# Turning q and k by DMA transposes from the sixth unit on, in a fused attention and Mish MLP kernel

## The chip, the cores and the metric

The kernel runs on one NeuronCore of a Trainium2 chip. The metric is the device time of one execution in microseconds (us), lower is better. A profile of one execution is read beside it; in it PE is TensorE (matmuls and transposes through the array), PEld its weight loads, DVE is VectorE, ACT is ScalarE, POOL is GpSimd, and SP is SyncE, which here only issues DMAs, one after the other in program order.

## The reference

Attention with one added to the softmax's denominator, followed by a two-layer network with the Mish activation. q, k and v have 8 batches, 12 heads, 448 rows and 64 columns.

```python
scores = scale * np.matmul(q, k.transpose(0, 1, 3, 2))
m = np.max(scores, axis=-1, keepdims=True)
e = np.exp(scores - m)
attn = e / (np.sum(e, axis=-1, keepdims=True) + np.exp(-m) + 1e-09)
attn_out = np.matmul(attn, v)
...
x = attn_out.transpose(0, 2, 1, 3).reshape(B * S, H * D)      # 3584 x 768
h = x @ w_in                                                  # 768 x 2048
sp = np.where(h > 20.0, h, np.log1p(np.exp(np.minimum(h, 20.0))))
out = (h * np.tanh(sp)) @ w_out                               # 2048 x 768
```

## The kernel before

The 12 heads of a batch are taken as 6 pairs (`HP`), so that 2 x 64 columns fill the 128 partitions, and there are 48 pairs in all (`N_PAIRS`). Three pairs make a unit (`UNIT_PAIRS`), two units a batch, 16 units the whole. The 448 rows of a head are loaded as 112 partitions with 4 row groups (`NT`, `SP_`).

For each pair, q, k and v are loaded by SP (`load_pair`, line 148, three DMAs of 224 KB) and cast to bf16 by POOL (`cast_pair`, lines 192 to 198, and `cast_v`, line 178). Then q and k have to be turned, so that the 64 columns of each head lie on partitions. `transpose_pair` (line 215) does that with eight PE transposes of 112 x 128 into PSUM, and `evac_qk` (lines 255 and 263) copies the two results into a tile `qkT` (DVE takes q and multiplies by the scale, ACT takes k). `turn_by_dma` (line 229) does it with two DMA transposes issued on SP instead, straight from the cast tiles to `qkT`; for such pairs the scale goes into the cast of q (line 194). `rest_of` (lines 237 and 238) then has POOL copy the last 64 rows of q of both heads into a small tile.

`scores` (lines 293 to 301) multiplies q with k, and DVE takes the row maxima (line 319). `exps` (line 330) is the exponential on ACT into the tile `en`. `denominators` and `normalise` (lines 343 to 366) divide: two pairs of a unit on DVE, the third on POOL (line 364). `normalise` also issues the DMA transpose of `en` into `eT` on SP (line 370), 128 x 3584 in bf16. `av_pair` (line 403) multiplies `eT` with v into `xT`. `mm1_mish` (lines 422 and 450) is the first layer with Mish into `gT`, and `mm2_part` (line 511) the second layer, whose results are copied out by DVE (line 498) and stored by SP (`store_rows`, line 476).

The order on each engine is the order in which the code emits instructions (`manual_schedule`). The main loop goes over units. A unit has a body of twelve steps, each with the exponentials of one score block, and between them the scores that come next, the products with v of the unit before, and pieces of the second layer, by a table written out by hand (`GROUPED`, line 553). In the body SP also gets the three pairs' loads (steps 0, 3 and 6, `LOAD_AT`) and the turns by DMA (steps 8 and 11, `TURN_AFTER`, line 704); POOL gets the casts of the first two of the next unit's pairs. After it comes a tail of eight steps, each with one block of the first layer: step 0 normalises the first pair, steps 1, 3 and 5 turn the next unit's three pairs on PE unless they are turned by DMA, step 1 casts the next unit's third pair, step 3 has `rest_of` for pairs turned by DMA and normalises the second pair, step 4 normalises the third on POOL, and step 7 emits the first scores of the next unit.

So SP sees for each unit: three transposes of `en`; then nine loads with two or four stores among them (their places repeat every four units); then, where pairs are turned by DMA, two transposes for each, the first pair's behind the last loads, the second's behind a store that may follow. `qkT` has three buffers, `eT` three, the cast q and k six, and `en` four.

Of the kernel before, what the change touches and what calls it, by code (L numbers as in the profile page):

```python
# [15 lines left out]
UNIT_PAIRS = 3  # L16
# [3 lines left out]
def kernel(  # L20
# [27 lines left out]
    N_PAIRS = B * HP  # L48
# [62 lines left out]

    GROUP_FROM = 2 * HP
    ONE_COPY = range(1, HP + UNIT_PAIRS)
    TURN_BY_DMA = (N_PAIRS - UNIT_PAIRS, N_PAIRS - UNIT_PAIRS + 1)
    SCALED_IN_CAST = (*ONE_COPY, *TURN_BY_DMA)
    q_rests = [
        singles.tile([128, 2, 64], BF16, tag=f"qr{i}", name=f"qr{i}") for i in range(UNIT_PAIRS)
# [53 lines left out]
    def load_w(n):  # L171
        for _ in range(min(n, len(pieces))):
            dst, src = pieces.popleft()
            nc.gpsimd.dma_start(out=dst, in_=src.rearrange("(a p) c -> p a c", p=128))
# [28 lines left out]
    def transpose_pair(p, bank=None):  # L203
        if p >= N_PAIRS:
            return
        q_bf, k_bf, _ = casted[p]
        ps = mo_take() if bank is None else sc_banks[2][bank]
        ps_k = sc_banks[1][bank] if bank is not None else mo_take() if p == 0 else ps
        by_s = [
            t[:, :].bitcast(BF16).rearrange("p (s n) -> p s n", s=2)[:, s, :]  # L210
            for s, t in enumerate((ps, ps_k))
        ]
        for s, src in enumerate((q_bf, k_bf)):
            for t in range(NT):
                nc.tensor.transpose(  # L215
                    by_s[s][:, t * SP_ : (t + 1) * SP_],
                    src[:, t].rearrange("p h d -> p (h d)"),
                    ident[:SP_, :SP_],
                )
        own = [] if bank is not None else [ps, ps_k] if p == 0 else [ps]  # L220
        if p in ONE_COPY:
            by_s = ps[:, :].bitcast(BF16).rearrange("p (s n) -> p s n", s=2)[:, :, 0:S]
        qkT[p] = (by_s, own)

    def turn_by_dma(p):
        qk = qk_pool.tile([128, 2, S], BF16, tag="qkT", name="qkT")
        pair = qk[:, 0, :], qk[:, 1, :]
        for dst, src in zip(pair, casted[p]):
            nc.sync.dma_start_transpose(
                out=dst.rearrange("c (t q) -> c t q", q=SP_),  # L230
                in_=src.rearrange("q t h d -> q (t h d)"),
            )
        qkT[p] = pair
# [115 lines left out]
    def normalise(p, dma=True, on_pool=False, shared=0):  # L349
        st = att[p]  # L350
        en = st["en"]
        by_pool = range(NTILE) if on_pool else range(shared)
        for i in [*(i for i in range(NTILE) if i not in by_pool), *by_pool]:
            pool_does = i in by_pool
            if pool_does and i == 0:

                st["rden2"] = st_pool.tile([128, NTILE], FP32, tag="rden2", name="rden2")
                nc.vector.tensor_copy(out=st["rden2"], in_=st["rden"])  # L358
            args = dict(
                out=en[:, :, i, 0:SP_], in0=en[:, :, i, 0:SP_],  # L360
                scalar1=st["rden2" if pool_does else "rden"][:, i : i + 1],
            )
            if pool_does:
                nc.gpsimd.tensor_scalar(scalar2=1.0, op0=ALU.mult, op1=ALU.mult, **args)  # L364
            else:
                nc.vector.tensor_scalar(scalar2=None, op0=ALU.mult, **args)  # L366
        eT = eT_pool.tile([128, NT, 2 * S], BF16, tag="eT", name="eT")
        st["eT"] = eT
        if dma:
            nc.sync.dma_start_transpose(  # L370
                out=eT.rearrange("c j (i q) -> c (j i) q", q=128),
                in_=en.rearrange("q j i c -> q (j i c)"),
            )
# [284 lines left out]
    for u in range(UNITS_PER_B, N_UNITS + 2 * UNITS_PER_B):  # L658
# [12 lines left out]
        for n in range(steps):  # L671
            pi, s = divmod(n, STEPS)
            p, idx = p0 + pi, p0 * STEPS + n
# [4 lines left out]
            if grouped:  # L678
# [23 lines left out]
                if u - UNITS_PER_B < len(W_AT):  # L702
                    load_w(W_AT[u - UNITS_PER_B].get(n, 0))
                if n in TURN_AFTER and nxt + TURN_AFTER.index(n) in TURN_BY_DMA:
                    turn_by_dma(nxt + TURN_AFTER.index(n))
# [40 lines left out]
        for f in range(FF_U):  # L746
# [20 lines left out]
            if f in (1, 3, 5):  # L767
                if nxt + f // 2 not in TURN_BY_DMA:
                    transpose_pair(nxt + f // 2, bank=f // 2 % 2)
# [7 lines left out]
            if f == 3:  # L777
                normalise(todo[1], dma=todo[1] not in BY_PE)
                for p in TURN_BY_DMA:
                    if p // UNIT_PAIRS == u + 1:  # L780
# [42 lines left out]
```

## Time and profile before

| | us |
|---|---|
| three runs | 462.74, 466.14, 467.04 (median 466.14) |
| the profiled execution, from its first to its last instruction | 465.8 |
| ACT busy in it | 347.0 |
| DVE busy | 338.1 |
| POOL busy | 184.9 |
| landing of a q, k, v load after its issue (median) | 4.9, 5.3, 5.4 |
| landing of an `eT` transpose (median of 43) | 6.7 |
| landing of a `qkT` transpose, q and k (median of 2 each) | 5.9, 4.7 |

Rows of the profile name line, engine and operation, then what is written and read, the shapes and the count. In a group's row follow busy time and the mean time of one in ns, then the engine's idle time before them and what ended it. In a timeline the first two numbers are start and length in us, and a row on SP ("SPq") is the time that the issue of a DMA took, not its transfer; idle time before an instruction and its cause stand in brackets at the end. A row of the stretches gives a window, its length, the busy time and instruction count of each engine (PE, PEld, DVE, ACT, POOL), the granted TensorE clock as a share, the DMA engines' busy share and GB/s. A line of forty digits gives the busy tenths in forty equal slices of the span.

### The profile page before, as it was taken

Reading aid. Unit: us, or ns where it says so; the run is one execution under the profiler, and the core shown is the slowest. Engines: PE = TensorE matmul, PEld = TensorE weight load, DVE = VectorE, ACT = ScalarE, POOL = GpSimd, SP = SyncE. Lnnn points to the kernel's source line nnn. Section 1 sums busy time; section 2 is a strip of 40 time slices with the busy share of each in tenths; the row PEclk is TensorE's granted clock in tenths of the full one; section 3 lists DMA queues with packets and bytes.
Section 4 is the critical chain, followed back from the end, with each engine's and each line's share of the span. In section 5 each row is a group of like instructions: output and inputs, shape, how many; then the busy total and the mean of one; then the engine's idle time right before and its main releaser. Section 6 shows DMA issues by size and latency. Waiting matters only on the chain.

```text
span 465.8 us, 8846 instructions
## 1 busy us (share of the span) xinstructions
PE 439.0 (94%) x3032; PEld 235.2 (51%) x3032; DVE 338.1 (73%) x728; ACT 347.0 (74%) x916; POOL 184.9 (40%) x352
## 2 busy tenths in 40 slices
PE   4587899899999999999999999999999999999996
PEld 2243545454445454645555554545454555555565
DVE  4899767878887878878796888788787979430121
ACT  5998877889796979889796969798887969311300
POOL 4666828362617253444536271625354350000000
PEclk9997699899999999999999999999999999999999
DMA  8999999998999999898999989999999995950213
GB/s 224 218 193 230 255 160 237 201 184 198 205 244 228 247 199 213 231 207 246 201 239 211 250 137 251 216 224 225 197 232 216 233 207 126 172 136 1 68 35 101
DMA packets 204300, 90.81 MB, mean 195 GB/s; under 512 B 160992, under 2 KB 200800, under 8 KB 204256
## 3 DMA queue, kind: packets, MB, share of 16 engines
q1 hardware_dynamic: 196672, 83.92, 84.0%
q0 software_dynamic: 7488, 6.29, 9.2%
q8 instruction: 23, 0.38, 0.3%
q14 instruction: 21, 0.17, 0.1%
q10 hardware_dynamic: 96, 0.05, 0.0%
HBM read 45.61 MB, written 11.01 MB: 122 GB/s over the span
## 4 chain that ended last, share of the span: by engine, by line
PE 76%; DVE 8%; ACT 7%; DMA 4%; issue 3%; POOL 1%; SPq 1%; POOLq 0%; ACTq 0%; DVEq 0%
PE mo L511 30%; PE mo L422 22%; PE b L403 6%; PE b L422 6%; DVE negm L319 6%; ACT en L330 6%; DMA k_f<-in_k_dram 4%; PE b L293 3%; PE sc L293 2%; PE sc L215 2%; PE b L215 1%; PE mo L403 1%; PE mo L301 1%; DVE eT L385 1%; PE mo L381 1%
## 5 line engine op out<-in xcount | busy, mean ns | idle before, releaser
L511 PE MATMUL mo<-w_out_sb,gT 128*128 128x384 bf16 (+1 forms) x896 | 141.5, 304 | 0.9 <-DVE o_sb L498 0.7
L422 PE MATMUL mo<-xT,w_in_sb 128*128 128x448 bf16 x600 | 125.6, 353 | 0.6 <-ACT gT L450 0.3
L511 PEld LDWEIGHTS <-gT 128*128 128x128 bf16 x896 | 80.2, 98 | 58.8 <-issue 20.2
L450 ACT ACTIVATE gT<-mo 128x448 bf16<-128x448 f32 x98 | 53.3, 544 | 69.7 <-PE mo L422 69.3
L422 PEld LDWEIGHTS <-w_in_sb 128*128 128x128 bf16 x768 | 71.7, 98 | 64.6 <-issue 6.7
L330 ACT ACTIVATE en<-sc,negm 128x448 bf16<-128x448 f32 x156 | 97.6, 640 | 7.4 <-DVE negm L319 6.1
L319 DVE TENSOR_REDUCE negm<-b 128x1 f32<-128x448 f32 x144 | 79.9, 617 | 22.2 <-PE b L296 22.2
L319 DVE TENSOR_REDUCE negm<-sc 128x2 f32<-128x896 f32 x84 | 84.5, 1018 | 7.0 <-PE sc L296 3.7
L330 ACT ACTIVATE en<-b,negm 128x448 bf16<-128x448 f32 x144 | 89.5, 650 | 0.0
L364 POOL TENSOR_SCALAR en<-en,rden 128x448 bf16<-128x448 bf16 x109 | 67.3, 635 | 33.0 <-DVE rden L358 22.8
L366 DVE TENSOR_SCALAR en<-en,rden 128x448 bf16<-128x448 bf16 x227 | 68.0, 370 | 0.7
L498 DVE COPY o_sb<-mo 128x384 f32<-128x384 f32 (+1 forms) x64 | 32.3, 504 | 48.3 <-PE mo L511 44.5
L192 POOL CAST q_bf<-q_f 112x512 bf16<-112x512 f32 x37 | 22.8, 617 | 97.8 <-DMA q_f<-in_q_dram 97.0
L293 PE MATMUL sc<-qkT 64*128 64x448 bf16 x72 | 29.3, 415 | 10.7 <-ACT en L330 10.1
L403 PE MATMUL b<-eT,v_bf 112*64 112x448 bf16 x304 | 35.8, 357 | 0.0
L422 PE MATMUL b<-xT,w_in_sb 128*128 128x448 bf16 x162 | 35.2, 353 | 0.0
L178 POOL CAST v_bf<-v_f 112x512 bf16<-112x512 f32 x48 | 29.8, 621 | 8.1 <-DMA v_f<-in_v_dram 7.6
L330 ACT ACTIVATION_READ_ACCUMULATOR en<-sc,negm 128x1 f32 x156 | 32.8, 210 | 0.0
L330 ACT ACTIVATION_READ_ACCUMULATOR en<-b,negm 128x1 f32 x144 | 32.4, 225 | 0.0
L198 POOL CAST k_bf<-k_f 112x512 bf16<-112x512 f32 x47 | 29.1, 618 | 7.9 <-DMA k_f<-in_k_dram 7.0
L403 PEld LDWEIGHTS <-v_bf 112*64 112x64 bf16 x384 | 19.9, 113 | 19.9 <-issue 13.2
L296 PE MATMUL sc<-qkT 64*128 64x448 bf16 x72 | 29.7, 420 | 0.0
(70 smaller groups left out, 489.5 us busy)
## 6 DMA issues: line engine op xcount, KB each, us to landing
q_f<-in_q_dram SPq DMA_DIRECT2D x48, 224.0 KB, 4.9
k_f<-in_k_dram SPq DMA_DIRECT2D x48, 224.0 KB, 5.3
v_f<-in_v_dram SPq DMA_DIRECT2D x48, 224.0 KB, 5.4
w_in_sb<-in_moe_w_in_dram POOLq DMA_DIRECT2D x12, 256.0 KB, 6.7
w_out_sb<-in_moe_w_out_dram POOLq DMA_DIRECT2D x8, 384.0 KB, 7.4
out_dram<-o_sb SPq DMA_DIRECT2D x7, 336.0 KB, 3.7
out_dram<-o_sb SPq DMA_DIRECT2D x8, 288.0 KB, 4.1
out_dram<-o_sb SPq DMA_DIRECT2D x8, 240.0 KB, 3.7
```

Of the source, the lines that this page charges most:

```text
L178: nc.gpsimd.tensor_copy(out=casted[p][2], in_=loaded.pop(p)[2])
L293: nc.tensor.matmul(sc[0][:, 0:S], lhsT=qT[0:64, qa : qa + 128], rhs=kA, start=True, stop=True)
L296: nc.tensor.matmul(sc[1][:, 0:S], lhsT=qT[64:128, qb : qb + 128], rhs=kB, start=True, stop=True)
L319: nc.vector.tensor_reduce(out=negm, in_=scored, axis=AX.X, op=ALU.max, negate=True)
L330: nc.scalar.activation(out=st["en"][:, :, c, 0:SP_], in_=sc[bk][:, 0:S].rearrange("q (j c) -> q j c", j=NT), func=AF.Exp, bias=st["negm"][ ...
L364: nc.gpsimd.tensor_scalar(scalar2=1.0, op0=ALU.mult, op1=ALU.mult, **args)
L366: nc.vector.tensor_scalar(scalar2=None, op0=ALU.mult, **args)
L403: nc.tensor.matmul(av[h * 64 : (h + 1) * 64, 0:S], lhsT=v_bf[:, h, j * D : (j + 1) * D], rhs=e_h, start=(j == 0), stop=(j == NT - 1),)
L422: nc.tensor.matmul(h_ps[:, 0:S], lhsT=w_in_sb[:, dm, ff * 128 : (ff + 1) * 128], rhs=xT[b][:, dm, :], start=(dm == 0), stop=(dm == DM_T - 1),)
L450: nc.scalar.activation(out=gT[b][:, ff, :], in_=h_ps[:, 0:S], func=AF.Mish)
L498: nc.vector.tensor_copy(out=o_sb[:, cols], in_=st["o"][:, 0:n_cols])
L511: nc.tensor.matmul(st["o"][:, 0:n_cols], lhsT=src[:, ff, c0 : c0 + 128], rhs=w_out_sb[:, ff, cols], start=(ff == 0), stop=(ff == FF_T - 1),)
```

## The change

One line. Before, only the first two pairs of the last unit are turned by DMA. Now the first two of every unit from the sixth on are; the third pair stays on PE, as do all pairs of the first five units. Because the tuple `SCALED_IN_CAST` is built from it, the q of those pairs gets its scale in the cast. In the tails ahead of those units the PE transposes and their copies are not emitted, and in the bodies four DMA transposes are added on SP.

```diff
     ONE_COPY = range(1, HP + UNIT_PAIRS)
-    TURN_BY_DMA = (N_PAIRS - UNIT_PAIRS, N_PAIRS - UNIT_PAIRS + 1)
+    TURN_BY_DMA = tuple(p for p in range(5 * UNIT_PAIRS, N_PAIRS) if p % UNIT_PAIRS < 2)
     SCALED_IN_CAST = (*ONE_COPY, *TURN_BY_DMA)
```

The places in the main loop that read it are unchanged:

```python
if n in TURN_AFTER and nxt + TURN_AFTER.index(n) in TURN_BY_DMA:      # body
    turn_by_dma(nxt + TURN_AFTER.index(n))
...
if f in (1, 3, 5):                                                    # tail
    if nxt + f // 2 not in TURN_BY_DMA:
        transpose_pair(nxt + f // 2, bank=f // 2 % 2)
        evac_qk(nxt + f // 2)
```

## The prediction

> **What bounds the kernel now.** I read the page first, then the stretches of two neighbouring units, then the timelines of the PE, the SyncE queue (SP) and POOL around the one place where the kernel already turns two pairs by DMA. A unit is three head pairs; its "body" is the twelve steps of lines 671 to 737, its "tail" the eight of lines 746 to 783, where the next unit's q and k are turned.
>
> ```profile
> PE 439.0 (94%) x3032; PEld 235.2 (51%) x3032; DVE 338.1 (73%) x728; ACT 347.0 (74%) x916; POOL 184.9 (40%) x352
> PE   4587899899999999999999999999999999999996
> q1 hardware_dynamic: 196672, 83.92, 84.0%
> ```
>
> The PE is full from about the eighth slice on, and the SP's DMA queue (q1) holds the 16 DMA engines for 84% of the span, so the second resource is not far behind the first. The stretches of a unit with all turns on the PE and of the last one, whose first two pairs go by DMA, show it closer:
>
> ```profile
> 343.04:368.54 25.50, 25.50 (x183) 13.51 (x181) 20.27 (x46) 21.58 (x58) 10.08 (x21) 1.00 1.05 230
> 368.54:393.25 24.71, 24.71 (x167) 12.73 (x165) 20.72 (x45) 20.69 (x56) 9.07 (x19) 1.00 1.01 171
> ```
>
> PE is busy for the whole of both (25.50 of 25.50, 24.71 of 24.71) at clock 1.00: it alone sets the pace, and DVE, ACT and POOL have slack of about 4 us and more. The second has 16 matmuls fewer and is 0.79 us shorter. PE's timeline gives the same by another way:
>
> ```profile
> 345.15 0.36 PE L215 MATMUL sc<-ident,q_bf 112*128 112x112 bf16 x4
> 345.35 0.36 PE L215 MATMUL b<-ident,k_bf 112*128 112x112 bf16 x4
> 345.54 1.30 PE L422 MATMUL mo<-xT,w_in_sb 128*128 128x448 bf16 x6
> ...
> 356.85 0.95 PE L403 MATMUL b<-eT,v_bf 112*64 112x448 bf16 x8
> ```
>
> Eight transposes of one pair hold PE from 345.15 to 345.54, 0.39 us; two pairs make 0.78.
>
> **The change, part by part.** Ten more tails, those of units 4 to 13 counted from 0, lose two pairs on PE each; the built program has 160 matmuls fewer on PE and 40 DMA transposes more on SP, so the change does what it says. *Gain:* 10 x 0.79 = 7.9 us, if nothing else becomes late; 465.8 - 7.9 = 457.9 of span.
>
> *Free edits.* The evacuations of the turned pairs go from DVE and ACT, which wait anyway; q is cast with the scale on POOL instead of without, at the same price (lines 194 and 192):
>
> ```profile
> L192 POOL CAST q_bf<-q_f 112x512 bf16<-112x512 f32 x37 | 22.8, 617 | 97.8 <-DMA q_f<-in_q_dram 97.0
> L194 POOL TENSOR_SCALAR q_bf<-q_f 112x512 bf16<-112x512 f32 x10 | 6.2, 615 | 16.8 <-DMA q_f<-in_q_dram 16.8
> ```
>
> *What is added* is those 40 DMA transposes, four in each of ten bodies, at the steps 8 and 11, and they stand on SP ahead of the three transposes of `en` (line 370), behind which the next loads stand. The last unit's own case shows the order that every unit will have:
>
> ```profile
> 346.60 13.64 SPq L370 DMA_TRANSPOSE eT<-en  x3
> 360.29 0.57 SPq L148 DMA_DIRECT2D q_f<-in_q_dram  x1
> ...
> 365.72 0.55 SPq L148 DMA_DIRECT2D v_f<-in_v_dram  x1
> 366.92 1.19 SPq L229 DMA_TRANSPOSE qkT<-q_bf  x1
> 368.20 1.21 SPq L229 DMA_TRANSPOSE qkT<-k_bf  x1
> 369.58 1.98 SPq L229 DMA_TRANSPOSE qkT<-q_bf  x1
> 371.65 1.21 SPq L229 DMA_TRANSPOSE qkT<-k_bf  x1
> 372.96 13.30 SPq L370 DMA_TRANSPOSE eT<-en  x3
> ```
>
> From one start of the `eT` transposes to the next, 346.60 to 372.96, are 26.36 us, while PE's round is 24.71. SP has no rest in it but 0.65 us before the first turn (366.27 to 366.92) and 0.17 before the third: 13.69 for `eT`, 5.98 for nine loads and two stores, 0.65, then 2.49, 0.17, 3.28 and 0.10. This is a ring of its own: `eT` issue, loads, their landing, the casts on POOL, the turns, the next `eT` issue. Once, at the end, it cost nothing, since there was slack in front of it; ten times in a row the excess adds up. So I cost the ring for each of the four kinds of unit, which differ in where the stores stand. A turned pair is put at 2.5 us (1.19 + 1.21 and the gaps, 366.92 to 369.41), `eT` at 13.47, and the idle of SP that only PE's own pace made is left out:
>
> ```profile
> 270.73 13.47 SPq L370 DMA_TRANSPOSE eT<-en  x3
> 284.25 0.57 SPq L148 DMA_DIRECT2D q_f<-in_q_dram  x1
> ...
> 290.21 0.46 SPq L148 DMA_DIRECT2D v_f<-in_v_dram  x1
> ```
> ```profile
> 308.96 1.01 SPq L476 DMA_DIRECT2D out_dram<-o_sb  x2
> ...
> 315.58 0.81 SPq L476 DMA_DIRECT2D out_dram<-o_sb  x2
> ...
> 317.50 0.46 SPq L148 DMA_DIRECT2D v_f<-in_v_dram  x1
> 321.18 4.21 SPq L370 DMA_TRANSPOSE eT<-en  x1
> ```
> ```profile
> 318.31 0.61 POOL L198 CAST k_bf<-k_f 112x512 bf16<-112x512 f32 x1
> ```
> ```profile
> 334.92 0.57 SPq L148 DMA_DIRECT2D q_f<-in_q_dram  x1
> ...
> 337.54 0.46 SPq L148 DMA_DIRECT2D v_f<-in_v_dram  x1
> 341.08 0.81 SPq L476 DMA_DIRECT2D out_dram<-o_sb  x2
> ...
> 342.90 0.56 SPq L148 DMA_DIRECT2D v_f<-in_v_dram  x1
> 343.56 0.87 SPq L476 DMA_DIRECT2D out_dram<-o_sb  x2
> ```
>
> - Kind of the unit at 360 (loads, stores, loads): 13.52 + 5.98 + 0.65 + 2.49 + 0.17 + 2.5 + 0.1 = 25.4.
> - At 284: loads and stores 284.25 to 290.67, 6.42; turn 2.5; two stores 0.81; turn 2.5; gaps 0.3; with 13.47: 26.0.
> - At 309: the second pair's k is cast at 318.31 + 0.61 = 318.92, which is 10.05 after the `eT` issue ended, and its turn can't go before; 13.47 + 10.05 + 2.5 + 0.1 = 26.1.
> - At 335: 3.08 (334.92 to 338.00), 2.38 (341.08 to 343.46), turn 2.5, stores 0.87, turn 2.5, gaps 0.1; with 13.47: 24.9. The idle 338.00 to 341.08 is a store that waits for PE's work, and goes when SP is late.
>
> After the first changed unit there are ten rounds, three at 24.9, three at 25.4, two at 26.0, two at 26.1: 255.1 us, against 10 x 24.71 = 247.1 of PE: SP falls behind by 8.0. The first changed unit adds its own delay: its loads end at 317.96 behind the store that PE paces, two turned pairs later it is 322.96, and `eT` went at 321.18: 1.8 late.
>
> *What is late next, and the slack.* `eT` is waited for by the first product with v (line 403). Issue to landing, by the tile's view in the stretches 346 to 360 and 372.9 to 386, was 6.4 us in the one unit and 7.1 in the next (middle value):
>
> ```profile
> DMA to landing us min/median/max: 6.1/6.4/6.7
> ```
> ```profile
> DMA to landing us min/median/max: 6.8/7.1/7.8
> ```
>
> 346.60 + 6.4 = 353.0 against 356.85: 3.8, less the 0.79 by which PE comes sooner, 3.0. The third pair, still turned on PE, has less:
>
> ```profile
> 372.57 0.67 POOL L198 CAST k_bf<-k_f 112x512 bf16<-112x512 f32 x1 [1.25 <-DMA k_f<-in_k_dram]
> 374.81 0.28 POOL L237 COPY qr<-qkT 64x64 bf16<-64x64 bf16 x1 [0.43 <-DMA qkT<-q_bf]
> 375.61 4.32 POOL L364 TENSOR_SCALAR en<-en,rden 128x448 bf16<-128x448 bf16 x7 [0.23 <-DVE rden L358]
> ```
> ```profile
> 375.39 0.36 PE L215 MATMUL b<-ident,k_bf 112*128 112x112 bf16 x4
> ```
>
> Its k is cast at 373.24, and PE turns it at 375.39: 2.1 us. A late load makes PE wait there first, so I take 2.1 as the slack. POOL has a new wait too: the copies of line 237 wait for the turned q (0.43 us at 374.81), and the normalising of the third pair (line 364) stands behind them. It ends at 379.93, and SP came to that transpose two `eT` issues after 372.96, at about 381.8, so 1.9 us cover it; SP late by x moves both alike.
>
> *Sum.* 8.0 + 1.8 - 2.1 = 7.7 us of PE waits, against 7.9 gained: -0.2. That holds with every turn at 1.2 us; one of the four took 1.98, 0.78 more. Counted for one unit in four, 10 x 0.78 / 4 = 2.0: **+1.8, 467.6 us of span**. The page shows no time around the span, and the median of the runs, 466.14, stands 0.3 above it, well inside the runs' own spread (462.74 to 467.04), so I put the span's sum at 467.5. Bounds: without the wait of the kind at 309 (25.0) and with the loads at 284 as quick as the others (25.5), 3.2 less than -0.2 gives 462.4; with each round 0.96 longer, as the measured 26.36 is over my 25.4, 9.6 more gives 475.2.
>
> A rule of the Trainium skill speaks against the change: the page "VectorE: DVE Perf Modes", section "The three transpose paths", gives 390 ns for a 128x128 block on TensorE and 1309 ns by DMA. The trace disagrees on both: 0.39 us was eight blocks on PE, and a DMA turn of four blocks held SP for 1.19 to 1.98 us. By the page's figure, an estimate, 16 blocks would hold the queue for 20.9 us a unit in place of 5.2 and end near 620 us; I give that 0.01.
>
> **The rivals.** *SP keeps up (0.18).* If the ring is at most 24.71 the whole gain stays: 458. For it: SP's issues alone, without the waits for landing and cast, come to about 13.5 + 4.5 + 1.5 + 4.9 = 24.4; the late stores then wait for nothing. Against it: the only round on record is 26.36. The Trainium skill, "Advanced Engine Details and Errata", section "X-Bar Transpose (TRN2)", has transposes as fast as other DMAs, at 350 to 400 GB/s, and would lead here; the trace speaks against that rate, since three `eT` of 0.92 MB each took 13.47 us to issue, 204 GB/s.
>
> *The ring at its measured length (0.25): slower.* All ten rounds at 26.36: 16.5 + 1.8 - 2.1 - 7.9 = +8.3, 474. The place is SP between the second pair's cast and the next `eT` issue. For it: this is the only measured value, with all nine loads queued ahead. Against: 0.78 of it is one long turn. Slower by 1% (4.7 us) needs 12.6 us of waits, so a mean round of 26.0 decides.
>
> *The clock (0.03).*
>
> ```profile
> 35.00:40.00 5.00, 3.03 (x24) 1.43 (x25) 4.93 (x9) 4.01 (x15) 3.18 (x6) 1.00 1.05 248
> 40.00:45.00 5.00, 3.62 (x21) 1.50 (x17) 4.11 (x9) 4.46 (x13) 4.43 (x8) 0.50 1.33 232
> ```
>
> After a stretch in which PE was busy for 3.03 of 5 us, the granted clock was 0.50 in the next. Should PE's new waits do that, a stretch of 5 us at half clock costs 2.5 in each of eight units, 20 more: 487. Waits of about 1 us in 25 are far smaller.
>
> *Nothing moves (0.01):* 466.
>
> **How the numbers follow.** The forecast, 467.5 with its own range 462.4 to 475.2, has 0.52. Full cover, 458, is the likely end below, and the long ring, 474, above; 460 to 475 leaves out some 0.1 on either side. About 1% is what a measurement of this kernel can tell: faster than 461.5 has the 0.18 and 0.02 of the forecast's low edge, 0.20; slower than 470.8 has 0.25, 0.04 for the clock and the page's figure, and 0.02 of the forecast's upper edge, 0.31; the rest, 0.49, is within 1%.
>
> **What would show it.** PE's unit at 24.71 us of work with waits of 0.5 to 1.5 us beside it, ahead of line 215 or 403, from the third changed unit on, released by POOL casts or by `eT`. SP's `eT` starts 25 to 26.4 us apart, with no rest before the stores of line 476. If `eT` starts come 24.7 apart, SP keeps up. If they come over 26 apart and the waits stand there, the slow rival holds. If PE waits ahead of line 293 for `qkT`, the turned tiles themselves are late, which I put later than the cast.

## The result and the profile after

| | before | after |
|---|---|---|
| median of 4 runs, us | 465.69 (462.74 to 467.04) | 482.43 (480.75 to 485.82) |
| ratio, 95% interval | | 1.0376 (1.0323 to 1.043) |
| profiled execution, time / span | span 465.8 | 481.04 / 478.8 |

The change made the kernel 3.8% slower, by 16.7 us in the medians and 13.0 in the spans. The page of after, in the order of the busy line, the digits of PE, SP's DMA queue, and the chain of waits by engine and by line:

```profile
PE 434.4 (91%) x2872; PEld 226.9 (47%) x2872; DVE 340.3 (71%) x708; ACT 339.9 (71%) x896; POOL 187.7 (39%) x352
...
PE   4596898899998999999798999999899999999996
...
q1 hardware_dynamic: 215872, 88.51, 89.0%
...
PE 49%; DMA 24%; ACT 9%; DVE 9%; issue 4%; SPq 3%; POOL 2%; DVEq 0%; ACTq 0%; POOLq 0%
PE mo L511 18%; DMA eT<-en 16%; PE mo L422 15%; ACT en L330 7%; DVE negm L319 6%; DMA k_f<-in_k_dram 4%; PE b L403 4%; PE b L422 4%; DMA q_f<-in_q_dram 2%; PE b L293 2%; PE sc L293 2%; SPq L148 1%; POOL k_bf L198 1%; DMA qkT<-k_bf 1%; SPq L476 1%
```

The same first line of the chain, of before:

```profile
PE 76%; DVE 8%; ACT 7%; DMA 4%; issue 3%; POOL 1%; SPq 1%; POOLq 0%; ACTq 0%; DVEq 0%
```

PE carried 76% of the chain before and carries 49% now. The share of the DMAs rose from 4% to 24%, and 16% is `eT<-en`, the transposes of the attention weights, which the change doesn't touch. The list of what PE waited for says the same (total us, times, longest):

```profile
PE sc L293 <- ACT en L330: 11.2, 14, 2.1
PE b L403 <- DMA eT<-en: 11.1, 11, 1.8
...
PE sc L215 <- POOL q_bf L192: 2.6, 2, 2.4
PE b L215 <- POOL k_bf L198: 1.5, 4, 0.7
...
PE sc L403 <- DMA eT<-en: 1.0, 1, 1.0
...
PE b L293 <- DMA qkT<-k_bf: 0.2, 1, 0.2
```

The first row stood in the list of before with 10.1 us; the wait for `eT` at line 403 is new, 12.1 us with its second form, and the casts that PE waits for at line 215, now late, add about 4. The turned tiles themselves, last row, are hardly ever late. PE's idle time grew by 17.6 us (44.4 of 478.8 against 26.8 of 465.8) and its busy time fell by 4.6: that is the 13.0.

Where `eT` comes from is the SyncE queue. The timeline of before's queue, at the first and at the last start of three `eT` transposes of a stretch of ten rounds:

```profile
117.89 14.62 SPq L370 DMA_TRANSPOSE eT<-en  x3
...
372.96 13.30 SPq L370 DMA_TRANSPOSE eT<-en  x3
```

The same of after, with parts of two rounds between them:

```profile
117.32 14.32 SPq L370 DMA_TRANSPOSE eT<-en  x3
...
133.41 2.79 SPq L476 DMA_DIRECT2D out_dram<-o_sb  x4
...
138.44 0.87 SPq L476 DMA_DIRECT2D out_dram<-o_sb  x2
...
146.44 13.70 SPq L370 DMA_TRANSPOSE eT<-en  x3
...
225.44 13.70 SPq L370 DMA_TRANSPOSE eT<-en  x3
239.19 0.57 SPq L148 DMA_DIRECT2D q_f<-in_q_dram  x1
...
241.81 0.46 SPq L148 DMA_DIRECT2D v_f<-in_v_dram  x1
244.65 0.81 SPq L476 DMA_DIRECT2D out_dram<-o_sb  x2
...
247.07 1.19 SPq L229 DMA_TRANSPOSE qkT<-q_bf  x1
248.37 1.22 SPq L229 DMA_TRANSPOSE qkT<-k_bf  x1
249.67 1.00 SPq L476 DMA_DIRECT2D out_dram<-o_sb  x2
250.77 1.40 SPq L229 DMA_TRANSPOSE qkT<-q_bf  x1
252.27 1.21 SPq L229 DMA_TRANSPOSE qkT<-k_bf  x1
253.57 13.72 SPq L370 DMA_TRANSPOSE eT<-en  x3
...
386.78 12.96 SPq L370 DMA_TRANSPOSE eT<-en  x3
```

Ten rounds took 255.07 us before and take 269.46 now, 14.4 more, a mean of 26.95. What lies ahead of them is 0.6 shorter, and what follows 0.8 (465.8 - 372.96 = 92.8 against 478.8 - 386.78 = 92.0): 14.4 - 0.6 - 0.8 = 13.0. So the whole loss in span lies in these ten rounds. Added up over the ten, SyncE issued for 13.33 us of `eT`, 4.99 of loads, 1.70 of stores and 5.04 of turns per round, 1.31 went into the gaps between issues, and it rested for 0.58, where before it had rested for 4.2. The queue is all but full.

### The profile page after: what moved, and what is told of

It is laid out like the page before. It is cut to its first block, busy times and chain, and to the rows that moved or that the text cites. A ratio compares the mean times of both kernels' runs of the same rounds, so it can differ in the third digit from the quotient of the medians.

```text
span 478.8 us, 8549 instructions
## 1 busy us (share of the span) xinstructions
PE 434.4 (91%) x2872; PEld 226.9 (47%) x2872; DVE 340.3 (71%) x708; ACT 339.9 (71%) x896; POOL 187.7 (39%) x352
## 4 chain that ended last, share of the span: by engine, by line
PE 49%; DMA 24%; ACT 9%; DVE 9%; issue 4%; SPq 3%; POOL 2%; DVEq 0%; ACTq 0%; POOLq 0%
PE mo L511 18%; DMA eT<-en 16%; PE mo L422 15%; ACT en L330 7%; DVE negm L319 6%; DMA k_f<-in_k_dram 4%; PE b L403 4%; PE b L422 4%; DMA q_f<-in_q_dram 2%; PE b L293 2%; PE sc L293 2%; SPq L148 1%; POOL k_bf L198 1%; DMA qkT<-k_bf 1%; SPq L476 1%
## 5 line engine op out<-in xcount | busy, mean ns | idle before, releaser
L511 PE MATMUL mo<-w_out_sb,gT 128*128 128x384 bf16 (+1 forms) x896 | 143.8, 307 | 0.9 <-DVE o_sb L498 0.7
L422 PEld LDWEIGHTS <-w_in_sb 128*128 128x128 bf16 x768 | 73.0, 98 | 69.4 <-issue 8.6
L366 DVE TENSOR_SCALAR en<-en,rden 128x448 bf16<-128x448 bf16 x227 | 73.3, 394 | 0.7
L194 POOL TENSOR_SCALAR q_bf<-q_f 112x512 bf16<-112x512 f32 x30 | 19.3, 643 | 134.7 <-DMA q_f<-in_q_dram 134.6
L293 PE MATMUL sc<-qkT 64*128 64x448 bf16 x72 | 28.8, 406 | 11.9 <-ACT en L330 11.2
L198 POOL CAST k_bf<-k_f 112x512 bf16<-112x512 f32 x47 | 30.9, 658 | 9.4 <-DMA k_f<-in_k_dram 8.4
L403 PEld LDWEIGHTS <-v_bf 112*64 112x64 bf16 x384 | 18.9, 111 | 32.4 <-DMA eT<-en 16.0
L412 DVE CAST xT<-b 128x448 bf16<-128x448 f32 x38 | 23.5, 619 | 14.1 <-PE b L403 12.7
```

Of the source, the lines that this page charges most:

```text
L198: cast_k(out=k_bf, in_=k_f.rearrange(by_t, t=NT))
L293: nc.tensor.matmul(sc[0][:, 0:S], lhsT=qT[0:64, qa : qa + 128], rhs=kA, start=True, stop=True)
L403: nc.tensor.matmul(av[h * 64 : (h + 1) * 64, 0:S], lhsT=v_bf[:, h, j * D : (j + 1) * D], rhs=e_h, start=(j == 0), stop=(j == NT - 1),)
L422: nc.tensor.matmul(h_ps[:, 0:S], lhsT=w_in_sb[:, dm, ff * 128 : (ff + 1) * 128], rhs=xT[b][:, dm, :], start=(dm == 0), stop=(dm == DM_T - 1),)
L511: nc.tensor.matmul(st["o"][:, 0:n_cols], lhsT=src[:, ff, c0 : c0 + 128], rhs=w_out_sb[:, ff, cols], start=(ff == 0), stop=(ff == FF_T - 1),)
```

## The experiments

The theory after the result: SyncE issues its DMAs in order, each issue takes time, and with four turns the round of issues is longer than PE's unit; `eT` stands last in the round, and PE waits for it. Rivals: PE's own work or its slower clock, the bytes of the turns on the DMA engines, or their landing.

### PE's work put back

All DMA turns stay, and the PE transposes that the change took away are made as well, into PSUM; their results are not used.

```diff
             if f in (1, 3, 5):
-                if nxt + f // 2 not in TURN_BY_DMA:
+                if nxt + f // 2 in TURN_BY_DMA[:-2]:
+                    by_dma = qkT[nxt + f // 2]
+                    transpose_pair(nxt + f // 2, bank=f // 2 % 2)
+                    qkT[nxt + f // 2] = by_dma
+                elif nxt + f // 2 not in TURN_BY_DMA:
```

> The changed kernel with the removed TensorE transposes put back in their places, into PSUM banks that nobody copies out; q and k are still taken from the DMA turns. TensorE's work per unit is 25.5 us again, SyncE's queue is as in the changed kernel. Theory, SyncE's queue sets the round: TensorE's waits of 1.6 us per unit swallow most of the 0.79, so 482 to 485. Rival, TensorE's own path still sets the round and its waits come on top: 7.9 us more than the changed kernel, 490.

Measured: 483.86 us, ratio to before 1.0385 (1.0318 to 1.0452); after had 482.43. PE is busy for 438.9 us, as before the change, and ten rounds take 270.5 (117.77 to 388.30). Some 8 us of PE work changed the time by 1.4, no more than the runs scatter: PE's work is not what sets the end any more, and the change would have lost about the same if its gain on PE had been nothing.

### One pair by DMA instead of two

```diff
-    TURN_BY_DMA = tuple(p for p in range(5 * UNIT_PAIRS, N_PAIRS) if p % UNIT_PAIRS < 2)
+    TURN_BY_DMA = tuple(p for p in range(5 * UNIT_PAIRS, N_PAIRS) if p % UNIT_PAIRS < 1 or p >= N_PAIRS - UNIT_PAIRS and p < N_PAIRS - 1)
```

> From the sixth unit on only the first pair of each unit is turned by DMA, the second again on TensorE (the last unit keeps two). Theory, the issue time of SyncE's queue sets the round: the ten rounds of the changed kernel, 26.95 us on the mean, lose one turned pair, 2.5 us, and come to 24.5, below TensorE's 25.1 (25.50 less 0.39); the queue keeps up, and the kernel is faster than before by 10 x 0.39 = 3.9 us: 462, with rounds of about 25.1 and almost no TensorE waits. Rival, each turn costs TensorE its own wait (late landing, or the DMA engines): half of the loss stays, 474.

Measured: 464.15 beside 466.93 of before, ratio 0.9944 (0.9905 to 0.9983). Its queue, first and last start of ten rounds:

```profile
114.53 13.82 SPq L370 DMA_TRANSPOSE eT<-en  x3
...
368.83 13.75 SPq L370 DMA_TRANSPOSE eT<-en  x3
```

25.43 us a round, about what PE needs with one pair less, 24.7 + 0.4 = 25.1. SyncE's issues and gaps fill 24.3 of it, near the 24.5 expected, and from 162 to 370 us PE waits only once for more than 0.3 us. Two turns a round fit, and the gain is there (3.9 by 10 x 0.39; 2.8 measured, by the interval 0.8 to 4.4); four don't.

### The same bytes in half as many issues

q and k of a pair are cast into one tile and turned by one DMA transpose of twice the size.

```diff
-        q_bf = bf_pool.tile([SP_, NT, 2, D], BF16, tag="q_bf", name="q_bf")
-        k_bf = bf_pool.tile([SP_, NT, 2, D], BF16, tag="k_bf", name="k_bf")
+        qk_bf = bf_pool.tile([SP_, 2, NT, 2, D], BF16, tag="qk_bf", name="qk_bf")
+        q_bf, k_bf = qk_bf[:, 0], qk_bf[:, 1]
+        both[p] = qk_bf
...
-        for dst, src in zip(pair, casted[p]):
-            nc.sync.dma_start_transpose(
-                out=dst.rearrange("c (t q) -> c t q", q=SP_),
-                in_=src.rearrange("q t h d -> q (t h d)"),
-            )
+        nc.sync.dma_start_transpose(
+            out=qk.rearrange("c s (t q) -> c (s t) q", q=SP_),
+            in_=both.pop(p).rearrange("q s t h d -> q (s t h d)"),
+        )
```

> The changed kernel with the cast q and k of a pair in one tile, and one DMA transpose for both in place of two: same bytes, same packets, two issues fewer in each round. Theory, issue time: a transpose of 448 rows of 256 bytes takes 1.2 us to issue and one of 3584 rows 4.27, so one of 896 takes 1.64; two of them with gaps save 1.7 us of the round, 26.95 to 25.25: about 466. Rival, the transposed bytes (DMA engines) are what costs: 480 to 484.

Measured: 467.89 beside 466.5, ratio 1.0059 (1.0022 to 1.0096). Line 229 in after, then in this kernel (duration of an issue in ns: least, median, longest; then first and last start):

```profile
L229 SPq DMA_TRANSPOSE qkT<-q_bf x22: 1183/1202/2405, 109.2 to 383.3; - x22
L229 SPq DMA_TRANSPOSE qkT<-k_bf x22: 1199/1212/1379, 111.7 to 385.5; - x22
```
```profile
L229 SPq DMA_TRANSPOSE qkT<-qk_bf x22: 1222/1470/3312, 108.6 to 371.3; - x22
```

1.47 us in the median in place of 1.20 + 1.21, for the same bytes. Its rounds, from the queue's timeline:

```profile
114.87 13.99 SPq L370 DMA_TRANSPOSE eT<-en  x3
...
373.16 13.21 SPq L370 DMA_TRANSPOSE eT<-en  x3
```

Ten take 258.29, 11.2 less than in after. With all bytes left, 14.5 us of the time are gone: the bytes of the turns are not the cause. I had expected 25.25 a round and got 25.83. Most of the difference is issue time again: the 20 transposes of the ten rounds took 1.92 us on the mean, not the 1.64 that I had reckoned, while SyncE rested 0.5 us a round, no more than in after. What makes single issues longer, up to 3.31 us, no run here shows.

### Issues without bytes

The kernel above, and behind each turn two loads of 256 bytes on SyncE, whose data nothing uses.

```diff
                     turn_by_dma(nxt + TURN_AFTER.index(n))
+                    for i in range(2):
+                        nc.sync.dma_start(
+                            out=small[2 * TURN_AFTER.index(n) + i], in_=moe_w_in[0:16, 0:4]
+                        )
```

> The kernel with one DMA transpose for each turned pair (467.9 us), and in each body with turns four more loads on SyncE, of 256 bytes each, two behind each turn: issues without bytes. Theory, SyncE's issue time: four issues of 0.40 to 0.46 us lengthen each round by 1.6 to 1.8, ten rounds by 16 to 18, with nothing to hide them: 480 to 486. Rival, the DMA engines' work is what fills the round: 11 KB in all cost nothing, 468.

Measured: 481.69 beside 465.69, ratio 1.0309 (1.0241 to 1.0377). The small loads' line and the queue:

```profile
L710 SPq DMA_DIRECT2D small<-in_moe_w_in_dram x44: 418/530/768, 113.5 to 389.2; - x44
```
```profile
120.05 14.06 SPq L373 DMA_TRANSPOSE eT<-en  x3
...
389.71 12.96 SPq L373 DMA_TRANSPOSE eT<-en  x3
```

Four issues of 0.53 us a round, 1 KB together, bring the round from 25.83 back to 26.97, that of after (26.95), and the time with it. Ten rounds are 11.4 us longer than without them; the other 2.4 of the 13.8 between the two medians lie outside these rounds. DMAs on SyncE's queue that move next to nothing are enough for the whole loss.

The issues do not simply add up, though. The small loads take 2.14 us a round, and the round grows by 1.14: the two turns take 2.90 a round here (median of one 1.26) in place of 3.84. So a part of an issue's duration is no fixed price; what that part waits for stays open.

### Loads taken off the queue

If SyncE is full, moving the loads of v elsewhere should free 1.5 us a round. Five kernels tried it, with the changed turns, with the turns of before as a control, and with the single turn per pair.

```diff
-            nc.sync.dma_start(
+            queue = nc.scalar if nm == "v" and p > 5 * UNIT_PAIRS else nc.sync
+            queue.dma_start(
```

By ScalarE, after and before:

> The changed kernel with the loads of v issued on ScalarE's queue from pair 16 on, so 32 issues fewer on SyncE's; bytes and transposes are the same. Theory, issue time of SyncE's queue: three issues of 0.5 us less in each round, 26.95 - 1.6 = 25.4, so ten rounds give back about 15 us: 467. Rival, the 16 DMA engines or the landing of the loads are full and not the queue: the same time as the changed kernel, 480 to 484.

> The kernel before with the same 32 loads of v on ScalarE's queue: what that move is worth or costs by itself. Theory: TensorE sets the pace before and ScalarE has 4 us of slack in a unit, so 466 within 1.5 us. Rival: ScalarE's exponentials become late by the 1.5 us of issues in each unit: up to 10 us slower.

By GpSimd (`nc.gpsimd` in the same place), after, before, and with one turn per pair:

> The changed kernel with the loads of v from pair 16 on issued on GpSimd's queue, which holds none of TensorE's, VectorE's or ScalarE's work. Theory, SyncE's issue time sets the round: three issues with their gaps, 0.6 us each, leave every round, 26.95 - 1.8 = 25.15, so ten rounds give back 15 to 18 us: 465 to 468. Rival, the DMA engines or the landings are full: 480 to 484, as the bytes are the same.

> The kernel before with the same loads of v on GpSimd's queue, as the control of that move. Theory: GpSimd waits 60% of the time and the issues (0.76 us each by the weight loads' rows) stand beside its casts: 466 within 2 us. Rival: the casts of q and k behind these issues become late for the TensorE transposes, up to 2 us a unit: 475 or more.

> One DMA transpose for each turned pair and the loads of v on GpSimd's queue together. Theory: the round on SyncE falls to 26.95 - 1.7 - 1.8 = 23.45, below TensorE's 24.71, so the whole of 7.9 us should come out: 458 to 460, faster than before. Rival, something beside SyncE's queue also holds the round (landing of the loads, the casts, the DMA engines): 464 or more.

| v loads on | turns of after | turns of before | one turn per pair |
|---|---|---|---|
| ScalarE | 491.0, 1.0521 (1.0433 to 1.0608) | 479.72, 1.0282 (1.0203 to 1.0361) | |
| GpSimd | 490.83, 1.054 (1.0486 to 1.0593) | 487.44, 1.046 (1.0394 to 1.0527) | 485.07, 1.0418 (1.0368 to 1.0467) |

All five miss their expectation by 13 to 25 us. The controls say why they can't judge the theory: without the change, the move alone costs 13 us (479.72 against 466.93) or 21 (487.44 against 466.5). The rival of the control on GpSimd had the size (475 or more) but not the place: PE waits there 18.9 us for `eT`, which it did not before, and about 3 for casts. Line 370 in before and, one line further down, in before with the v loads on GpSimd, and one round's three transposes there:

```profile
L370 SPq DMA_TRANSPOSE eT<-en x43: 4154/4332/6393, 19.6 to 405.5; - x43
```
```profile
L371 SPq DMA_TRANSPOSE eT<-en x43: 4080/4647/9847, 19.9 to 426.3; - x43
```
```profile
281.57 16.52 SPq L371 DMA_TRANSPOSE eT<-en  x3
```

The middle issue of an `eT` grew by 0.3 us, the longest by 3.5, and three took 16.52 where before took 13.47; landing went from 6.7 to 7.3 us (medians). Over ten rounds (120.59 to 394.10) the `eT` issues took 151.5 us in place of 136.6, 14.9 of the 21. A load that SyncE issues stands behind the transposes in the queue; on another queue it can run beside them, and the transposes get longer. Why they do was not tried. The Trainium skill, page "DMA: Bandwidth & Descriptors", section "Issuing engines are not separate DMA queues", says that DMAs of all issuing engines share the same 16 engines and interleave, so that a second queue saves only issue time, "usually small relative to the DMA itself". The first half fits the longer transposes; the second does not fit this kernel, where the issues of a round together are the bound.

### Both pairs in one DMA

q and k of both pairs in one tile and one transpose behind step 11.

```diff
+    qk_two = qk_pool.tile([128, 2, 2, S], BF16, tag="qk_two", name="qk_two", bufs=1)
...
-        for dst, src in zip(pair, casted[p]):
...
+        nc.sync.dma_start_transpose(
+            out=qk_two.rearrange("c i s (t q) -> c (i s t) q", q=SP_),
+            in_=both[p].rearrange("q i s t h d -> q (i s t h d)"),
+        )
```

> From the sixth unit on both turned pairs of a unit go in one DMA transpose (four tensors, 1792 rows of 256 bytes), issued at step 11: same bytes, one issue a round in place of four. Theory, issue time: the ten rounds of the kernel with one DMA a pair, 25.83 us on the mean, lose another fixed part of 0.8 to 1.0 and come to 25.0 or less, near TensorE's 24.71: 459 to 462, faster than before. Rival, the turned tiles now land too late for the first scores, or the bytes count: 466 or more.

Measured: 471.81 beside 465.69, ratio 1.0118 (1.0076 to 1.016), a miss. Its queue, then POOL beside it (idle before and its cause in brackets):

```profile
267.93 0.46 SPq L150 DMA_DIRECT2D v_f<-in_v_dram  x1
271.50 1.61 SPq L238 DMA_TRANSPOSE qk_two<-qk_bf  x1
273.21 13.74 SPq L380 DMA_TRANSPOSE eT<-en  x3
```
```profile
269.92 0.72 POOL L206 TENSOR_SCALAR qk_bf<-q_f 112x512 bf16<-112x512 f32 x1 [2.27 <-DMA q_f<-in_q_dram]
270.83 0.64 POOL L210 CAST qk_bf<-k_f 112x512 bf16<-112x512 f32 x1 [0.20 <-DMA k_f<-in_k_dram]
```

The issue of all turns took 1.61 us here, but SyncE rests 3.11 us ahead of it (268.39 to 271.50) until the second pair's k, cast at 271.47, is there, and `eT` stands behind it. This is one of the shortest issues; all of them, by the tile's view:

```profile
L238 SPq DMA_TRANSPOSE qk_two<-qk_bf x11: 1587/2767/3363, 110.3 to 374.3; - x11
```

Over ten rounds (116.87 to 377.23, 26.04 each) the one issue took 2.62 us on the mean, 1.2 less than the two of the kernel with one DMA a pair, but the rests grew from 0.5 to 2.1 us a round. The ring has a second limit, load, landing, cast and turn: less issue time is of use only down to that. It is the wait that I had counted for the unit at 309, and here both pairs' turns stand behind it.

### The best of both

One pair by DMA, with one DMA transpose for its q and k.

```diff
+    TURN_BY_DMA = tuple(p for p in range(5 * UNIT_PAIRS, N_PAIRS) if p % UNIT_PAIRS < 1 or p >= N_PAIRS - UNIT_PAIRS and p < N_PAIRS - 1)
...
+        nc.sync.dma_start_transpose(
+            out=qk.rearrange("c s (t q) -> c (s t) q", q=SP_),
+            in_=both.pop(p).rearrange("q s t h d -> q (s t h d)"),
+        )
```

> From the sixth unit on one pair a unit is turned by DMA, as one DMA transpose (the last unit keeps two pairs). Theory: the round on SyncE is under TensorE's 25.1 us with 1.5 to spare, so TensorE's gain of 3.9 us stands without the waits that the kernel with one pair in two DMAs (464.15 beside 466.93) still showed in its first and last changed units: 461 to 463. Rival, these waits come from the landing of the loads and not from issues: 463 to 465, as that kernel.

Measured: 463.15 beside 465.69, ratio 0.9937 (0.9906 to 0.9967), the lowest median of all kernels here. It lies just above the theory's range and at the low end of the rival's, and against two issues for that pair (0.9944) the ratio shows no difference. Ten rounds take 252.03 us (120.41 to 372.44), in which SyncE rests 2.3 us a round: where the queue has room, saved issues bring nothing that these runs can tell.

### A later start

The turns begin at the seventh unit, or at the eighth, the latter beside a second run of after.

```diff
-    TURN_BY_DMA = tuple(p for p in range(5 * UNIT_PAIRS, N_PAIRS) if p % UNIT_PAIRS < 2)
+    TURN_BY_DMA = tuple(p for p in range(6 * UNIT_PAIRS, N_PAIRS) if p % UNIT_PAIRS < 2)
```

> The changed kernel with the turns from the seventh unit on, so that the unit with six stores, whose round took 29.1 us on SyncE, holds no turns. Theory, issue time: that round alone was 4.4 us over TensorE's 24.71, less the slack of about 2 and the 0.79 of gain lost: 480 or a little less, some 1 to 4 us under the changed kernel. Rival, the round was long for a reason that follows the first turned unit wherever it stands: no less than the changed kernel.

> The changed kernel with the turns from the eighth unit on. The kernel from the seventh unit still had turns in the body with six stores (that body turns for the seventh unit; its round was 29.5 us again), so it did not take out what was meant; this one does. Theory, issue time: the eight rounds that stay between changed units take 215 us on SyncE against 197.7 of TensorE, less about 2 of slack and 6.3 of gain in eight tails: about 10 over the kernel before, 475, and some 5 to 8 under the changed kernel. Rival, the first turned unit is long wherever it stands, or the time does not follow the rounds' sum: at most 2 us under the changed kernel.

> The changed kernel itself once more, on the chip and in the rounds of the kernel from the eighth unit on, as its measure: 480 to 484.

From the seventh: 480.45, ratio 1.0296 (1.0227 to 1.0364). The expectation miscounted: a body turns the pairs of the unit behind it, so the body with six stores (133.41 and 138.44 in after's queue) still turns two, and its round was 29.52 again. From the eighth, where it turns none: 478.42, 1.0249 (1.0188 to 1.031), beside 481.72, 1.0348 (1.0278 to 1.0417), of after. That is 3.3 us for two rounds less, between the 5 to 8 of the theory and the 2 of the rival. The intervals overlap, so the size is rough, and this pair of kernels decides nothing by itself. The queue of this kernel shows what came back:

```profile
235.61 0.46 SPq L148 DMA_DIRECT2D v_f<-in_v_dram  x1
239.91 0.81 SPq L476 DMA_DIRECT2D out_dram<-o_sb  x2
```

SyncE rests 3.84 us ahead of a store whose rows PE, late itself, had not delivered; that round is 30.22 long (219.10 to 249.32). Part of it is the clock's: PE had waited 2.90 us for `eT` until 227.42, and the granted clock was 0.65 and 0.66 in the ten us from 225 on.

## Why the prediction was wrong

The forecast was 467.5 us and no change; it came out at 482.43, above the range.

**The step that failed is the term of the sum "ten rounds: 255.1 us".** Measured: 269.46, 14.4 more; in the profile of after's second run 269.15 (114.95 to 384.10). The mechanism was the right one, the ring of `eT`, loads, casts and turns on SyncE; its size was wrong. By the kinds of the prediction, the rounds came out like this:

| kind | counted | measured | more |
|---|---|---|---|
| at 335 | 3 x 24.9 | 29.12, 28.13, 26.64 | 9.2 |
| at 284 | 2 x 26.0 | 26.84, 27.24 | 2.1 |
| at 309 | 2 x 26.1 | 26.75, 27.18 | 1.7 |
| at 360 | 3 x 25.4 | 25.41, 26.34, 25.81 | 1.4 |

The kind that I took for the shortest is the longest. Two errors are in it. The first of the three rounds has six stores, not the two or four that I took every body to have, in one batch of 2.79 us and one of 0.87, and I cost that body by a later one: 4.2 us, of which the stores make 2.0 (3.66 against 1.68) and a longer `eT` 0.9 (14.32 against 13.47). In the second, the wait for a store that I left out, since it "goes when SP is late", stood there with 2.38 us (242.27 to 244.65): PE waits for `eT` too, so the store that it paces is late with the queue and doesn't get ahead of it. In the second profile the same wait was 1.11 us (241.30 to 242.41). The other 7.8 us are spread over the ten: rests of less than 1 us each, 3.4 in all, and issues and gaps some tenths longer than those that I had taken them from.

**The first changed unit's own delay, 1.8,** did not come: the first `eT` of the ten rounds starts at 117.32, not later than the 117.89 of before, after a rest of SyncE from 115.70 on. Without this term the working gives 269.5 - 247.1 - 2.1 - 7.9 = +12.4, against 13.0 in the span. So the slack and the gain on PE were about right together; that they agree to some tenths is luck, as the second profile's span is 475.9.

**The time around the span.** I put it at 0.3 us; the profiled execution of after took 481.04 for a span of 478.8, so it is 2.2. In the runs of before that were taken beside the experiments it is 1.7 to 2.1, so this term was too small for both kernels. The rest of the distance is the scatter of the runs: 481.04 is the profiled run, the median is 1.4 above.

**Where the wait stands.** I expected it ahead of line 215 first. It is mainly at line 403, in eight of the ten rounds, once or, as here, twice (PE's timeline of after):

```profile
231.76 0.95 PE L403 MATMUL b<-eT,v_bf 112*64 112x448 bf16 x8 [0.79 <-DMA eT<-en]
...
238.00 0.95 PE L403 MATMUL b<-eT,v_bf 112*64 112x448 bf16 x8 [1.70 <-DMA eT<-en]
```

Six of these 11 waits stand at the first product of a unit (5.8 us in all), three at the second (3.8) and two at the third (1.5). The five later ones all follow an `eT` that landed 7.8 to 8.2 us after its issue, where the median is 6.5: the one here was issued at 229.78. Before had such landings too (one of 8.0 in the round at 194), and the slack hid them.

The slack of the first `eT` I had read in the wrong unit. The 3.0 came from the `eT` of 346.60, which has no turns ahead of it in its round. The `eT` of 372.96, which has, landed 7.1 us later, at 380.1, and its product stood here (PE's timeline of before):

```profile
381.56 0.95 PE L403 MATMUL b<-eT,v_bf 112*64 112x448 bf16 x8
```

That is a slack of 1.5, less than the 2.1 of the cast, so PE waits at line 403 first, and once it has, the cast in the tail is mostly in time. That the turned tiles are not late (line 293, 0.2 us) held.

**The rivals.** "SP keeps up" fell: no round is as short as 24.71. The ring at its measured length had the right side, the right place and its sign, rounds over 26 with the waits beside them; its 474 was low since the mean is 26.95, not 26.36. One round on record, the only one that showed the whole sequence, was better evidence than my four rebuilt from parts, and I had corrected it downward. The clock rival did occur, in three units; here are two and one without (stretches of after):

```profile
137.34:167.61 30.27, 26.96 (x169) 13.06 (x167) 19.91 (x43) 20.85 (x56) 12.03 (x23) 0.94 1.08 235
218.26:247.97 29.71, 26.54 (x165) 12.79 (x164) 22.89 (x45) 21.14 (x56) 14.38 (x27) 0.94 1.09 228
355.28:380.86 25.58, 24.52 (x166) 12.51 (x165) 20.76 (x43) 20.63 (x56) 10.70 (x21) 1.00 1.08 232
```

PE's work takes 2.0 to 2.4 us longer at 0.94. It does not set the end: after's second profile has two such units and the same ten rounds (269.15), the kernel with four small loads has the rounds of after and 481.69 us with no unit under 1.00 in its ten rounds, and the one with PE's work put back has one such unit and 483.86. A part of the 2.38 us for which the store came late may be the clock's: where it was 1.11, the clock of that round was 1.00.

## What to carry to other kernels

Treat an engine that issues DMAs in order as a resource like any other: write down its whole round, every issue with its duration and gap, and compare it with the round of the engine that sets the pace, for every kind of unit, the irregular ones too. If it is close, fewer and larger DMAs buy room, and moving work onto that queue pays only up to the room left: one pair here, not two. A wait that "goes" when the waiting engine is late stays if the engine that it waits for becomes late with it; and a load moved to another queue needs its control, since here it cost more than it freed.

## What was not expected of the hardware

- An issue on SyncE took nearly the same for 256 bytes (median 0.53 us) as for a load of 224 KB (mostly 0.46 to 0.57); a transpose of twice the bytes took 1.47 us, or 1.26 in the kernel with small loads (medians), in place of 2 x 1.2. Single issues took longer, a load up to 1.5 us and such a transpose up to 3.3.
- With loads issued from another queue, the issue of the transposes on SyncE was longer (from GpSimd median 4332 to 4647 ns, longest 9847), and the kernel lost 13 us from ScalarE and 21 from GpSimd.
- A wait of PE of 1.7 us can be followed by half clock. Stretches of after behind the wait that ended at 238.00 (the granted clock is the third number from the end):

```profile
238.00:240.00 2.00, 2.00 (x13) 0.98 (x14) 0.62 (x1) 1.18 (x4) 0.00 (x0) 0.83 1.27 290
240.00:242.00 2.00, 2.00 (x8) 0.41 (x7) 1.12 (x2) 0.73 (x2) 0.00 (x0) 0.50 0.90 244
242.00:244.00 2.00, 2.00 (x12) 0.96 (x10) 1.72 (x4) 1.84 (x6) 0.99 (x2) 0.82 0.98 240
```

A drop of 0.17, 0.50 and 0.18 from full clock over three stretches of 2 us is 0.85 x 2 = 1.7 us lost, or 3.4 us at half clock. The two other waits of after's ten rounds that are as long, 2.37 us (until 145.41) and 1.83 (until 261.69), are followed by the same loss, and none of those up to 1.36 is. It is no fixed threshold: in after's second profile a wait of 1.75 us (until 237.16) leaves the clock at 1.00. The Trainium skill, page "TensorE: Matmul & The Clock Gate", section "What's actually happening", has the clock at half after at least one idle window of about 3.4 us, and at full again after about 3.4 us of sustained work. The 3.4 us at half clock agree with the second; that 1.7 us of waiting were enough does not fit the first.
